# Block-sparse attention with a gated output: gathers moved behind both pairs' value products, query scaling moved behind the divisions

## The chip, the cores and the metric

One core of a Trainium2 chip. The metric is the device time of one execution in microseconds (us). The engines named below are TensorE (PE in the profile; PEld is its weight loads), VectorE (DVE), ScalarE (ACT), GpSimd (POOL) and SyncE (SP), which only issues transfers.

## The reference, cut to what matters

Batch 4, 8 heads, 768 positions, head size 64. Positions are in 24 blocks of 32. A block of queries sees the first and the last block, its own and both neighbours, and three blocks drawn at random; blocks 0 and 23 see everything.

```
scores = (q @ k^T) / 8, masked blockwise
attn   = softmax(scores)
x      = attn @ v                                  # heads side by side: 512 columns
gate   = sigmoid(causal convolution of x, 5 taps, one filter for each column)
out    = (gate * (x @ w_val)) @ w_out              # 512 x 512 weights
```

## The kernel before, in words

**Pairs and units.** The 22 inner query blocks of a batch are taken as 11 pairs of two neighbouring blocks. Blocks 0 and 23 form one more pair, the global one (`pr.glob`), which is worked in two halves. A unit is an inner pair or a half of a global one, 13 to a batch and 52 in all. `pr.seq` counts the inner pairs, 0 to 43.

**A unit's work.** `scores` multiplies the pair's queries (`qc`) by twelve blocks of keys (`kg`), takes the maxima on VectorE (`mx`) and the exponentials on ScalarE (`pe`). One step later `transposes` turns the exponentials on TensorE and ScalarE copies them out (`ptr`). `values` multiplies these by the values: `va` holds the first and last block and the pair's own two, which SyncE loads; `vb` holds, for each of the two query blocks, its other neighbour and its three drawn blocks, which POOL fetches by two indirect transfers of 128 rows (the gathers, `load_values`). The products go to `av`. VectorE then divides them by the row sums (`rs`, `x`). `finish` transposes the quotients (`xp`) into `xT`. A pair from batch 2 or 3 has 32 small products of values, each with 32 columns of weights and 65 columns of output; the profile shows each as two matmul records, 64 for a pair. In batches 0 and 1 (`wide`) pairs of products are joined where they can be, and there are 48 records.

**The gated output** runs in the gaps: `gates` (convolution on VectorE, tile `th`), `split` (`xh`, `xl`), and `project`, which issues on TensorE twelve products into `vp` for each quarter of the columns, evicts them by VectorE (`y`, `yl`) and ScalarE (`yh`), and then issues the output products `op`, in lots of six. The strings `FILLS` and `STEPS` say how many lots of TensorE work (`fill`) and of VectorE work (`prepare`) go in behind each transposed tile.

**Order.** Each engine is wrapped in `InOrder`, so its instructions run in the order in which the program issues them. Up to unit 21 a step takes one unit. From `DOUBLE_AT` = 22 on (the while loop at line 791) a step takes two inner units at once, or one unit around a global pair. Such a step is, in the program's order:

1. scale the queries of the next step's units (line 798, `SCALE_AHEAD` = 2), in place, on ScalarE for batches 0 and 1 and on VectorE for batches 2 and 3;
2. issue stores that are ready (SyncE);
3. scores of this step's units, with maxima and exponentials;
4. loads of later queries and keys (SyncE), and copies of keys into `kg` (POOL, and others) for the units of the next step;
5. values of the units of the step before (`to_value`), each with its division on VectorE;
6. value loads for the pairs three further on (`VRING` = 3): SyncE for `va`, POOL for the gathers;
7. further loads of queries and keys, transposes of this step's units with lots of projection and gate work between them, and the transposes of the quotients.

The buffers that set the waits: `vb` has three, so the gathers of pair s + 3 write the buffer that the products of pair s read. In a two-unit step, then, the two gathers of the first pair loaded wait for the first pair's products, and the two of the second for the second's. `va` and `kg` are rings of three and four, `qc` has five buffers.

Of the kernel before, what the change touches and what calls it, by code (L numbers as in the profile page):

```python
# [35 lines left out]
SCALE_AHEAD = 2  # L36
# [27 lines left out]
def attention_moe(ctx, tc, qb, kb, v, ve, sampled, w_val, conv_w, w_out, ident_in, slot_in, out):  # L64
# [29 lines left out]
    pe, dve, act, pool, sp = (InOrder(e) for e in (nc.tensor, nc.vector, nc.scalar, nc.gpsimd, nc.sync))  # L94
    matmul, transpose = pe.matmul, pe.transpose
# [55 lines left out]
    def indices(b):  # L151

        row = const.tile([128, NB], F32, tag=f"row{b % 2}", name="row")
        dve.tensor_scalar_add(row, base, float(b * S - B * S))
        dve.tensor_tensor(out=row, in0=row, in1=valid, op=ALU.mult)
        dve.tensor_scalar_add(idx[:, b, :], row, float(B * S))
# [18 lines left out]
    def run(calls):  # L175
        while calls:
            calls.pop(0)()
# [160 lines left out]
    def load_values(pr):  # L338
        b = pr.bt.b
        if pr.glob:  # L340
            return
        if pr.p == 0 and b:
            indices(b)
        vt = va[pr.seq % VRING]
        pr.va = vt
        if pr.p < VRING:
            sp.dma_start(vt[0 : 2 * BLK, :], ve[b])
        i0 = PAIRS[pr.p][0]
        sp.dma_start(vt[64:128, :], v[b * S + i0 * BLK : b * S + (i0 + 2) * BLK, :])
        pr.vb = three.tile([128, 2, H * DV], F32, tag="vb", name="vb")  # L350
        for j, i in enumerate(PAIRS[pr.p]):
            pool.indirect_dma_start(
                out=pr.vb[:, j, :], out_offset=None, in_=v,
                in_offset=bass.IndirectOffsetOnAxis(ap=idx[:, b, i : i + 1], axis=0),
            )


    class Unit:
# [65 lines left out]
    def transposes(un, places=((ps_pt, "pt"),) * 3):  # L424
        un.PT = []
        for p, (space, tag) in zip(un.P, places):
            pt = space.tile([128, 4, 128], F32, tag=tag, name="pt")
            for c in range(4):
                transpose(pt[:, c, :], p[:, 128 * c : 128 * c + 128], ident)
            t = five.tile([128, 4, 128], F32, tag="ptr", name="ptr")  # L430
            act.copy(t, pt)
            un.PT += [t[:, c, :] for c in range(4)]
            yield

    def values(un, second=False):
        pr = un.pr
        if un.e == 0 and second:
            pr.av = ps_pt.tile([128, 512], F32, tag="pt", name="av")[:, 0 : 4 * DV].rearrange(
                "p (a h d) -> p a h d", a=2, h=2
            )  # L440
        elif un.e == 0:
            pr.av = ps_av.tile([128, 2, 2, DV], F32, tag="av", name="av")
        if pr.glob:
            for h in range(2):
                for c in range(6):
                    pt = un.PT[4 * h + c if c < 4 else 4 + 2 * h + c]
                    for hp in range(HP):
                        cols = slice(BLK * hp, BLK * hp + BLK)
                        hd = 2 * hp + h
                        matmul(  # L450
                            pr.av[cols, un.e, h, :], pt[:, cols], pr.bt.vn[:, c, hd * DV : (hd + 1) * DV],
                            start=c == 0, stop=c == 5, tile_position=(0, BLK * hp),
                        )
        else:
            slots = [(a, h, b, (4 * a + 2 * b + h) * DV) for a in range(2) for h in range(2) for b in range(2)]
            wide = pr.bt.b < WIDE
            if wide:
                for a, h, b, hd in slots:
                    matmul(
                        pr.av[64 * b : 64 * b + 64, a, h, :], un.PT[4 * h + 2 * a][:, 64 * b : 64 * b + 64],  # L460
                        pr.va[:, hd : hd + DV], start=a + h == 0, stop=False, tile_position=(0, 64 * b),
                    )
            for a, h, b, hd in slots:
                for c in range(1 if wide else 0, 2):
                    for j in range(2):
                        rows = slice(64 * b + BLK * j, 64 * b + BLK * j + BLK)
                        vt = pr.vb[:, j, :] if c else pr.va
                        matmul(
                            pr.av[rows, a, h, :], un.PT[4 * h + 2 * a + c][:, rows], vt[:, hd : hd + DV],
                            start=c == 0, stop=a + h == 2 if wide else c == 1, tile_position=(0, rows.start),  # L470
                        )
        if un.last:
            rs = three.tile([128, 2, 2, 2], F32, tag="rs", name="rs")
            dve.tensor_scalar_add(rs[:, 0], pr.av[:, :, :, D], 1e-9)
            dve.reciprocal(rs[:, 1], rs[:, 0])
            pr.x = two.tile([128, 2, 2, D], F32, tag="x", name="x")
            dve.tensor_tensor(
                out=pr.x, in0=pr.av[:, :, :, 0:D], in1=rs[:, 1, :, :, None].to_broadcast([128, 2, 2, D]), op=ALU.mult
            )
# [163 lines left out]
    def store():  # L643
        while stores:
            sp.dma_start(*stores.pop(0))
# [30 lines left out]
    def fill(times=1):  # L676
        for _ in range(times):
            if may_project():
                run(late)
                advance(to_project)  # L680
# [21 lines left out]
    def freed(k):  # L702

        return units[min(k, N - 1)].pr.seq if k >= 0 else -1

    def more(which, upto, load):
        if at[which] < len(pairs) and pairs[at[which]].seq <= upto:
            load(pairs[at[which]])
            at[which] += 1
            return True  # L710

    def until(which, n, do):
        while at[which] < min(len(pairs), pairs.index(units[min(n, N - 1)].pr) + 1):
            do(pairs[at[which]])
            at[which] += 1
# [7 lines left out]
    for n in range(DOUBLE_AT):  # L723
# [5 lines left out]
        def more_values():  # L729
            return more("values", freed(n - LAG_V - 1) + VRING, load_values)  # L730
# [57 lines left out]
    to_value = units[DOUBLE_AT - LAG_V : DOUBLE_AT - LAG_T]  # L788
    to_finish = [un.pr for un in units[DOUBLE_AT - LAG_X : DOUBLE_AT - LAG_V] if un.last]
    n = DOUBLE_AT  # L790
    while n < N or to_turn or to_value or to_finish:
        step[0] = n
        now = units[n : n + 1]
        if n > DOUBLE_AT and len(units[n : n + 2]) == 2 and not any(un.pr.glob for un in units[n : n + 2]):
            now = units[n : n + 2]
        n += len(now)
        last = n - 1
        until("scaled", last + SCALE_AHEAD, scale)
        store()
        for i, un in enumerate(now):  # L800
            scores(un, i == 1)
        while now and more("keys", now[0].pr.seq + RING, load_keys):
            pass
        until("copied", last + COPY_AHEAD, copy_keys)
        for i, un in enumerate(to_value):
            values(un, i == 1)
            if un.last:
                to_finish.append(un.pr)
        if to_value:
            while more("values", to_value[-1].pr.seq + VRING, load_values):  # L810
                pass
        while more("keys", freed(last) + RING, load_keys):
            pass
        run(waiting)
        run(copies)

        def finish_pairs():
            if not to_finish:
                return
            xp = ps_pt.tile([128, 4, 128], F32, tag="pt", name="xp")  # L820
            ends = [finish(pr, xp[:, 2 * i : 2 * i + 2, :]) for i, pr in enumerate(to_finish)]
            for _ in range(2):
                for end in ends:
                    next(end, None)
            to_finish.clear()

        to_turn += now
        places = [(ps_sc, "sc")] * 3 + [(ps_pt, "pt")]
        count, done = sum(len(un.P) for un in to_turn), 0
        if len(to_turn) < 2:  # L830
            k = units.index(to_turn[0]) if to_turn else last + 1
            fill(int(FILLS[2 * k]))
            finish_pairs()
        for un in to_turn:
            k = units.index(un)
            step[0] = k
            for half, _ in enumerate(transposes(un, places[done : done + len(un.P)])):
                done += 1
                if done == count:
                    finish_pairs()  # L840
                at_half = 2 * k + min(half, 1)
                if len(to_turn) > 1 or half:
                    fill(int(FILLS[at_half]))
                prepare(int(STEPS[at_half]))
        to_value, to_turn = to_turn, []
# [54 lines left out]
```

## Time and profile before

| | |
|---|---|
| median of 3 runs | 402.89 us (402.58 to 407.91) |
| the profiled execution | 405.32 us, span 403.6 us |
| TensorE busy | 359.4 us (89%) |
| VectorE busy | 268.5 us (67%) |
| ScalarE busy | 255.5 us (63%) |
| POOL busy | 143.0 us (35%) |
| mean granted TensorE clock | 0.977 |
| chain of waits | TensorE 63%, VectorE 12%, issue 8%, ScalarE 7%, transfers 6% |
| gathers (vb) on POOL | 88, mean 983 ns |

Busy time is a share of the whole span. The chain of waits follows the work that ended last back to the start; "issue" in it is time in which an engine waited for nothing that the profile shows. A timeline row gives the start of its first instruction, the time from there to the end of its last, the engine, the line (of a helper, so always 82), the operation and its tiles, how many instructions the row holds, and in brackets the idle time of the engine ahead of them and what ended it. Matmuls are pipelined: a row of four can begin before the row ahead of it has ended. [...]

### The profile page before, as it was taken

Reading aid. Unit: us, or ns where it says so; the run is one execution under the profiler, and the core shown is the slowest. Engines: PE = TensorE matmul, PEld = TensorE weight load, DVE = VectorE, ACT = ScalarE, POOL = GpSimd, SP = SyncE. Lnnn points to the kernel's source line nnn. Section 1 sums busy time; section 2 is a strip of 40 time slices with the busy share of each in tenths; the row PEclk is TensorE's granted clock in tenths of the full one; section 3 lists DMA queues with packets and bytes.
Section 4 is the critical chain, followed back from the end, with each engine's and each line's share of the span. In section 5 each row is a group of like instructions: output and inputs, shape, how many; then the busy total and the mean of one; then the engine's idle time right before and its main releaser. Section 6 shows DMA issues by size and latency. Waiting matters only on the chain.

```text
span 403.6 us, 15476 instructions
## 1 busy us (share of the span) xinstructions
PE 359.4 (89%) x6274; PEld 286.4 (71%) x6274; DVE 268.5 (67%) x618; ACT 255.5 (63%) x619; POOL 143.0 (35%) x237
## 2 busy tenths in 40 slices
PE   8788889799789899697889988898999988999995
PEld 7356666566557788496668976696778867989794
DVE  4345798776978695375838856756755966779640
ACT  1958788788779567255648567755655866564521
POOL 1885656485733333503241051513351043000000
PEclk9989999999989999979989999999999999999999
DMA  7988966899944455968753676797660374101102
GB/s 229 302 287 262 325 224 169 229 297 320 306 141 103 123 153 114 298 207 236 218 148 104 175 185 165 210 310 218 188 185 18 89 203 137 53 28 54 52 26 81
DMA packets 52584, 72.37 MB, mean 179 GB/s; under 512 B 6944, under 2 KB 34720, under 8 KB 52512
## 3 DMA queue, kind: packets, MB, share of 16 engines
q1 hardware_dynamic: 44896, 47.69, 39.9%
q0 software_dynamic: 7040, 23.43, 20.1%
q8 instruction: 50, 0.82, 0.9%
q10 hardware_dynamic: 576, 0.24, 0.2%
q14 instruction: 22, 0.18, 0.2%
HBM read 65.05 MB, written 6.29 MB: 177 GB/s over the span
## 4 chain that ended last, share of the span: by engine, by line
PE 63%; DVE 12%; issue 8%; ACT 7%; DMA 6%; SPq 2%; POOL 1%; ACTq 0%; POOLq 0%; DVEq 0%
PE vp L82 14%; PE op L82 14%; PE av L82 14%; PE pt L82 10%; PE sc L82 7%; DVE mx L82 3%; DVE th L82 3%; PE s L82 3%; PE xp L82 2%; DMA qc<-in_q 2%; SPq L82 2%; ACT ptr L82 2%; DMA k<-in_k 2%; ACT pe L82 2%; DMA vb<-in_v,idx 2%
## 5 line engine op out<-in xcount | busy, mean ns | idle before, releaser
L82 POOL DMA_INDIRECT vb<-in_v,idx x88 | 86.5, 983 | 166.8 <-PE av L82 124.1
L82 DVE SCALAR_TENSOR_TENSOR th<-xT,cw,th 128x384 f32<-128x384 f32 x128 | 79.4, 629 | 24.5 <-ACT th L82 19.1
L82 ACT ACTIVATE pe<-sc,mx 128x256 f32<-128x256 f32 x176 | 67.9, 487 | 37.4 <-DVE mx L82 31.3
L82 ACT COPY ptr<-pt 128x512 f32<-128x512 f32 x112 | 64.2, 604 | 36.9 <-PE pt L82 28.4
L82 DVE TENSOR_REDUCE mx<-sc 128x2 f32<-128x512 f32 x88 | 55.5, 684 | 28.2 <-PE sc L82 16.9
L82 POOL COPY kg<-k 128x256 f32<-128x256 f32 (+1 forms) x143 | 55.9, 430 | 32.7 <-PE sc L82 24.0
L82 PE MATMUL av<-va,ptr 128*32 128x65 f32 (+1 forms) x1056 | 46.2, 226 | 11.7 <-issue 9.9
L82 PE MATMUL sc<-kg,qc 64*32 64x256 f32 x1408 | 52.5, 391 | 4.1 <-DVE rs L82 1.3
L82 PEld LDWEIGHTS av<-va,ptr 128*32 128x32 f32 (+1 forms) x1056 | 34.7, 118 | 29.5 <-issue 21.4
L82 PE MATMUL av<-vb,ptr 128*32 128x65 f32 x1408 | 44.0, 222 | 12.3 <-issue 11.0
L82 PE MATMUL op<-wo,yh 128*128 128x512 f32 x192 | 54.6, 407 | 0.1
L82 PE MATMUL pt<-ident,pe 128*128 128x128 f32 x352 | 51.5, 282 | 2.4 <-ACT pe L82 1.7
L82 PE MATMUL vp<-xh,wv 128*128 128x384 f32 x256 | 52.9, 349 | 0.0
L82 PEld LDWEIGHTS pt<-ident,pe 128*128 128x128 f32 x352 | 41.7, 144 | 8.1 <-ACT pe L82 2.5
L82 PEld LDWEIGHTS vp<-xh,wv 128*128 128x128 f32 x256 | 45.4, 193 | 0.3
L82 PEld LDWEIGHTS av<-vb,ptr 128*32 128x32 f32 x1408 | 32.8, 109 | 17.7 <-issue 14.5
L82 PEld LDWEIGHTS sc<-kg,qc 64*32 64x32 f32 x1408 | 27.1, 108 | 21.1 <-issue 9.6
L82 PEld LDWEIGHTS op<-wo,yh 128*128 128x128 f32 x192 | 35.4, 192 | 7.6 <-ACT yh L82 0.5
L82 ACT CAST yh<-y 128x384 fp32r<-128x384 f32 x32 | 16.5, 517 | 24.2 <-DVE y L82 23.0
L82 PE MATMUL op<-wo,yl 128*128 128x512 f32 x96 | 31.5, 409 | 0.0
L82 PE MATMUL vp<-xl,wv 128*128 128x384 f32 x128 | 28.0, 341 | 0.0
L82 DVE SCALAR_TENSOR_TENSOR y<-th,vp 128x384 f32<-128x384 f32 x32 | 17.6, 549 | 14.6 <-PE vp L82 14.6
(68 smaller groups left out, 433.2 us busy)
## 6 DMA issues: line engine op xcount, KB each, us to landing
kg<-in_k SPq DMA_DIRECT2D x165, 64.0 KB
vn<-in_v SPq DMA_DIRECT2D x12, 520.0 KB
qc<-in_q SPq DMA_DIRECT2D x48, 128.0 KB
k<-in_k SPq DMA_DIRECT2D x12, 512.0 KB
out<-ot SPq DMA_DIRECT2D x23, 256.0 KB
va<-in_v SPq DMA_DIRECT2D x44, 130.0 KB
wst<-in_w_val SPq DMA_DIRECT2D x4, 512.0 KB
wst<-in_w_out SPq DMA_DIRECT2D x4, 512.0 KB
```

Source lines behind the costliest of these rows:

```text
L82: made = getattr(self.eng, name)(*args, **kwargs)
```

## The change

In a two-unit step the first gather is made to wait for the last matmul of the step's value products, that is for the second pair's too; the other gathers of the step stand behind it on POOL. `product` keeps the last value matmul issued, and `valued` hands it to the first gather of the step and is then cleared. Where only one unit's values are computed in a step, and in the steps of one unit before unit 22, nothing changes for gathers. The scaling of the next step's queries moves from the head of the step to behind the value loads, so that on its engine it comes behind this step's maxima (or exponentials) and behind the divisions. No work is added or taken away.

```
--- before.py
+++ after.py
@@ load_values
         for j, i in enumerate(PAIRS[pr.p]):
-            pool.indirect_dma_start(
+            made = pool.indirect_dma_start(
                 out=pr.vb[:, j, :], out_offset=None, in_=v,
                 in_offset=bass.IndirectOffsetOnAxis(ap=idx[:, b, i : i + 1], axis=0),
             )
+            if valued[0] is not None:
+                tc.add_manual_dep(
+                    made.ins, valued[0].name,
+                    mybir.DependencyInfo(mybir.DependencyClass.Sync, mybir.DependencyReason.DATA),
+                    reason="behind the value products",
+                )
+                valued[0] = None
@@ values (in both branches)
+    valued, product = [None], [None]
...
-                        matmul(
+                        product[0] = matmul(
...
-                        )
+                        ).ins
@@ the loop of two-unit steps
         n += len(now)
         last = n - 1
-        until("scaled", last + SCALE_AHEAD, scale)
         store()
         for i, un in enumerate(now):
             scores(un, i == 1)
...
         if to_value:
+            valued[0] = product[0] if len(to_value) > 1 else None
             while more("values", to_value[-1].pr.seq + VRING, load_values):
                 pass
+            valued[0] = None
+        until("scaled", last + SCALE_AHEAD, scale)
         while more("keys", freed(last) + RING, load_keys):
             pass
```

## Rows read from the trace of the kernel before

**Rows 1.** Waits of TensorE, 130 to 360 us: total us, times, longest.

```profile
PE av L82 <- issue: 17.3, 35, 2.7
```

**Rows 2.** Timeline of TensorE in one two-unit step.

```profile
230.58 0.33 PE L82 MATMUL av<-va,ptr 128*32 128x65 f32 x8
...
232.62 0.22 PE L82 MATMUL av<-va,ptr 128*32 128x65 f32 x1 [0.16 <-issue]
...
234.09 0.33 PE L82 MATMUL av<-va,ptr 128*32 128x65 f32 x4 [0.43 <-issue]
...
234.82 0.33 PE L82 MATMUL av<-vb,ptr 128*32 128x65 f32 x4 [0.40 <-issue]
...
235.08 0.66 PE L82 MATMUL pt<-ident,pe 128*128 128x128 f32 x4
...
235.50 1.64 PE L82 MATMUL vp<-xh,wv 128*128 128x384 f32 x8
```

**Rows 3.** Timeline of POOL, 150 to 404 us: gathers.

```profile
157.23 0.97 POOL L82 DMA_INDIRECT vb<-in_v,idx  x1 [11.99 <-issue]
...
232.06 0.97 POOL L82 DMA_INDIRECT vb<-in_v,idx  x1 [12.23 <-PE av L82]
...
235.42 0.95 POOL L82 DMA_INDIRECT vb<-in_v,idx  x1 [1.15 <-PE av L82]
```

**Rows 4.** Timeline of TensorE, four other places.

```profile
152.55 0.69 PE L82 MATMUL av<-va,ptr 128*64 128x65 f32 x16
...
154.98 0.66 PE L82 MATMUL pt<-ident,pe 128*128 128x128 f32 x4
...
158.68 1.03 PE L82 MATMUL pt<-ident,pe 128*128 128x128 f32 x8
...
176.43 1.63 PE L82 MATMUL vp<-xh,wv 128*128 128x384 f32 x8
...
352.07 0.34 PE L82 MATMUL av<-va,ptr 128*32 128x65 f32 x8
...
354.04 1.66 PE L82 MATMUL op<-wo,yh 128*128 128x512 f32 x6
```

**Rows 5.** Timeline of TensorE: value products and next work, two steps.

```profile
183.99 0.33 PE L82 MATMUL av<-va,ptr 128*32 128x65 f32 x8
...
189.01 0.66 PE L82 MATMUL pt<-ident,pe 128*128 128x128 f32 x4
...
336.17 0.33 PE L82 MATMUL av<-va,ptr 128*32 128x65 f32 x8
...
340.41 0.60 PE L82 MATMUL pt<-ident,pe 128*128 128x128 f32 x4 [0.41 <-issue]
```

**Rows 6.** Timelines of VectorE and TensorE around 200 us.

```profile
199.92 0.15 DVE L82 TENSOR_SCALAR rs<-av 128x4 f32<-128x4 f32 x1
...
200.32 0.42 DVE L82 TENSOR_TENSOR x<-av,rs 128x256 f32<-128x256 f32 x1
...
203.79 1.82 PE L82 MATMUL pt<-ident,first 128*128 128x128 f32 x8
```

**Rows 7.** Timeline of TensorE, two steps around 135 and 165 us.

```profile
135.68 0.69 PE L82 MATMUL av<-va,ptr 128*64 128x65 f32 x16
...
140.35 1.64 PE L82 MATMUL vp<-xh,wv 128*128 128x384 f32 x8
...
164.56 0.69 PE L82 MATMUL av<-va,ptr 128*64 128x65 f32 x16
...
170.82 1.97 PE L82 MATMUL pt<-ident,pe 128*128 128x128 f32 x8 [1.70 <-ACT pe L82]
```

**Rows 8.** Timeline of VectorE, 120 to 172 us: one scaling.

```profile
169.00 0.29 DVE L82 TENSOR_SCALAR qc<-qc 128x256 f32<-128x256 f32 x1 [6.15 <-DMA qc<-in_q]
```

**Rows 9.** Busy us of PE, PEld, DVE, ACT, POOL; then clock, DMA share, GB/s.

```profile
163.00:182.10 19.10, 15.45 (x205) 14.15 (x205) 9.81 (x23) 8.12 (x19) 4.60 (x7) 0.82 0.86 247
182.10:195.30 13.20, 10.48 (x230) 8.89 (x230) 8.46 (x19) 8.25 (x20) 4.92 (x6) 1.00 0.82 238
```

More of the change, by code (lines that the diff above doesn't have):

```diff
@@ L467, in values @@
                         vt = pr.vb[:, j, :] if c else pr.va
-                        matmul(
+                        product[0] = matmul(
                             pr.av[rows, a, h, :], un.PT[4 * h + 2 * a + c][:, rows], vt[:, hd : hd + DV],
                             start=c == 0, stop=a + h == 2 if wide else c == 1, tile_position=(0, rows.start),
-                        )
+                        ).ins
         if un.last:
```

## The prediction

> **What bounds the kernel now.** I read the chain of waits first. Through the two-unit steps it is one run of TensorE work with short pieces called "issue" in it, so there whatever delays TensorE delays the end. The waits of TensorE alone, between 130 and 360 us, say what these pieces are: 17.3 us of idle time ahead of value products (av), with nothing named that it waited for; every other wait there is under 2 us in total, and none is for gathered rows [rows 1]. The timeline of TensorE then shows where in a step they lie. In the step whose value products begin at 230.58 the first pair and most of the second go through at full pace; a first gap ends at 232.62, and from there three or four products come at a time, 0.73 us apart (234.09 to 234.82), until the transposes begin at 235.08 [rows 2]. Beside it the reader should lay the timeline of POOL: the first gather of this step starts at 232.06, just ahead of that first gap [rows 2, 3].
>
> Two stretches decide whether the gather is the cause. In the step at 352.07 there is nothing left to gather: the products of two pairs (128 records) take 354.04 - 352.07 = **1.97 us**. In the step at 152.55 the gathers are late (they wait for new indices and start at 157.23): two pairs of the wide form take **2.43 us** [rows 3, 4]. Neither has a gap. In the other steps the same work takes 4.2 to 5 us. And what gathers do beside sparse work is there as well: gathers 3 and 4 of the 230.58 step run from 235.42 beside eight projections that take 1.64 us, against 1.63 us for eight at full clock with no gather [rows 2 to 4]; and under the four gathers from 157.23 eight transposes take 1.03 us [rows 3, 4]. So a gather costs TensorE only where TensorE issues very short products one upon the other.
>
> **The change part by part.**
>
> *Gathers behind the last value product.* It takes gathers 1 and 2 out of the second pair's products in eleven steps (the twelfth is the one at 152.55, already without them). Price of each: from the first value product to the next work, less the undisturbed time. Nine steps of 128 such records lie between 183.99 and 336.17: the first loses 189.01 - 183.99 - 1.97 = 3.05, the last 340.41 - 336.17 - 1.97 = 2.27, all nine 23.6 us [rows 5]. One of them can't give it all. At 197.69 TensorE goes straight to transposing the quotients, and those come from VectorE: it starts the first division at 199.92, each of two takes 0.82 us (to 200.74 for the first), so TensorE has them at 201.6 and its next transposes begin near 201.85 instead of 203.79, a gain of 1.9 and not 2.9 [rows 6]. That leaves 22.7. The step at 135.68 loses 140.35 - 135.68 - 2.43 - 0.42 (four transposes, as from 235.08 to 235.50) = 1.8 [rows 2, 4, 7]. Subtotal **24.5 us**.
>
> What the new wait holds up: behind the waiting gather stand, on POOL, the other three and then key copies. The first gather moves from 1.5 us after the first product (230.58 to 232.06) to about 2.3 us (1.97 and the 0.34 that gather 3 shows behind its product's end), so 0.8 us later against the step's start; the fourth ends about when it does today, since gathers 3 and 4 wait for the second pair already. Their rows are used one step on, a whole step later (the steps of rows 9 last 13 to 19 us), and by the program the copies behind them are for keys read at the scores of the step after the next. I cost this at nothing; the cover is that step of distance, and if it went, TensorE would wait for gathered rows, which it does nowhere after 130 us [rows 1, 3].
>
> *Queries scaled behind the maxima and divisions.* The scaling issues no DMA; SyncE's stores and key loads, POOL's copies and the value gathers, past which it moves in the program, run on other queues and keep their order. On VectorE 0.29 us for each query leaves the stretch ahead of the maxima and lands behind the divisions, ahead of the evictions of projections. In most steps both places are hidden under TensorE. In one, it decides: VectorE stood 6.15 us for a query load at 169.00 with the step's maxima behind it, so the exponentials came late and TensorE, done with its products, waited for them until 170.82 [rows 7, 8]. With the change those maxima run at once. The products begin at 164.56; one wide and one short pair take 2.2 us, so the transposes come near 166.8: **4.0 us** gained, gaps included. [...] Without the idle time I expect no fall, **2.6 us** more [rows 2, 4, 7, 9].
>
> *What is late next.* The ceiling is 24.5 + 4.0 + 2.6 = 31.1 us. Two things take from it. First, VectorE: the maxima and the first division now end while the products stand in their gaps; without them the second division (0.82) has to follow the first, and the scaling (0.29 to 0.6) comes behind it, so evictions start about 1 us later against the end of the products [rows 6, 8]. In two steps (183.99 and 230.58) output products follow one projection later and need its eviction: I take 0.5 each, **1.0** (bounds 0 and 2). Second, the transfers: from 163.00 to 195.30 the DMA engines are busy 0.86 x 19.1 + 0.82 x 13.2 = 27.2 us, and this stretch would shrink from 32.3 to 22.6 [rows 9]. Loads are issued a step ahead, so part of the missing 4.6 us can be carried into the emptier stretch behind; bounds 0 and 4.6, I take **3.0**, since both windows are near full.
>
> Sum: 31.1 - 1.0 - 3.0 = **27 us**. The profiled execution (405.32 us, span 403.6) would become 378; it lies 2.4 us above the median of 402.89, so the forecast is **376 us**.
>
> **The rivals.**
>
> *A. The gaps stay (0.10).* The slow stretch could belong to a long run of short products, which uses up what was issued ahead, and fall together with the gather by the fixed order of the step. For it: both begin at the same place of nearly every step. Against: the two undisturbed stretches, of which one has all 128 [rows 4]. It isn't excluded, because that one follows a single unit's scores instead of two. Then only the step at 164.56 gains: the 1.70 us that TensorE stood ahead of 170.82, with the clock 4.3; **399 us** [rows 7]. [...]
>
> *B. Half of it comes back as other waits (0.16).* The four gathers, now in one row, slow the first transposes: at the pace of [rows 2], four in 0.73 us, eight transposes take 1.45 instead of 0.84, 0.6 in each of twelve steps, 7 us; and the transfers take their full 4.6. With VectorE's 1.0 this leaves 31 - 13 = 18; **385 us**. For it: the full DMA windows [rows 9]; against it, transposes and projections at full pace beside gathers [rows 2, 4].
>
> *C. Slower (0.03).* In its new place the scaling waits for its query load with the evictions behind it; TensorE then waits for evicted projections in place of issue gaps. Price up to the 6.15 us of [rows 8] each. It decides once this wait exceeds about 2.9 us in all twelve steps (27 lost and 8 more); **411 us**. Against it: the new place is 4 us later, and one wait of that size is found.
>
> *D. No new wait arises (0.01).* If the first gather already stood behind both pairs nothing would move. But gathers 1 and 3 start 3.4 us apart, one behind each pair [rows 3].
>
> **How the numbers follow.** Forecast 0.70, from 368 (the ceiling of 31, and 3 more if the step at 197.69 also keeps its clock and its quotients are early) to 383. With B to 389 the range holds somewhat over 8 in 10; A, C and D and the worst of B lie outside. A measurement here can tell about 2%, 8 us, from no change: the limit is 395. Forecast and B are faster, 0.86; A and D within, 0.11; C slower, 0.03.
>
> **What would show it.** In the trace after, value products of two pairs should take about 2 us in every two-unit step, with the first gather starting 0.3 us behind them and TensorE's issue time at value products between 130 and 360 us below 5 us. The four gathers should stand back to back, with projections of 1.64 us beside them. [...] The forecast is wrong if the gaps stay with no gather beside them (A), if they reappear at transposes, or if TensorE now waits for vb, kg or evictions (B, C).

## The result and the profile after

The change takes the median from 405.94 us (402.58 to 409.13) to **394.11 us** (392.62 to 398.94), five executions each: a ratio of 0.972, 95% interval [0.967, 0.977]. It is faster, by 11.8 us where 27 were forecast, and outside the range of 368 to 389. The profiled execution of after took 398.94 us (span 397.1, granted clock 0.973) and is the longest of the five; its rows are read below for what happens, the medians for how much. Ratios, here and below, compare the executions of each kernel that lie within 1.5% of its fastest, so they can differ from the ratio of the medians.

The idle time that the change was to remove is nearly gone. TensorE's waits between 130 and 360 us in after (total us, times, longest), the first two rows:

```profile
PE av L82 <- DMA va<-in_v: 12.0, 4, 3.7
PE av L82 <- issue: 2.1, 2, 1.6
```

The issue time at value products fell from 17.3 us to 2.1 [rows 1], as forecast. But the row above it is new: 12.0 us, in four waits, for the values that SyncE loads.

A step in the middle, in TensorE's timeline of after (start, time to the last end, engine, line, operation, count, idle time ahead of it):

```profile
224.93 0.33 PE L82 MATMUL av<-va,ptr 128*32 128x65 f32 x8
...
226.91 0.66 PE L82 MATMUL pt<-ident,pe 128*128 128x128 f32 x4
227.32 1.63 PE L82 MATMUL vp<-xh,wv 128*128 128x384 f32 x8
```

and POOL's beside it:

```profile
227.31 0.97 POOL L82 DMA_INDIRECT vb<-in_v,idx  x1 [13.13 <-PE av L82]
228.58 1.32 POOL L82 DMA_INDIRECT vb<-in_v,idx  x1 [0.30 <-issue]
230.21 1.29 POOL L82 DMA_INDIRECT vb<-in_v,idx  x1 [0.30 <-issue]
231.81 0.95 POOL L82 DMA_INDIRECT vb<-in_v,idx  x1 [0.30 <-issue]
...
240.46 0.97 POOL L82 DMA_INDIRECT vb<-in_v,idx  x1 [5.66 <-PE av L82]
```

The products of both pairs take 226.91 - 224.93 = 1.98 us here. That is the only one of the nine steps of 128 records in the sum where they do: in the other eight they take 2.70 to 6.42 us, with other waits in place of the old gaps. The four gathers stand in one row behind both pairs, and the projections beside the first two take 1.63 us for eight, as without a gather [rows 2 to 4]. The step near 163 us also went as forecast; TensorE and, below, VectorE:

```profile
162.76 0.69 PE L82 MATMUL av<-va,ptr 128*64 128x65 f32 x16
164.96 1.09 PE L82 MATMUL pt<-ident,pe 128*128 128x128 f32 x8
165.81 1.64 PE L82 MATMUL vp<-xh,wv 128*128 128x384 f32 x8
...
167.97 1.56 PE L82 MATMUL vp<-xh,wv 128*128 128x384 f32 x8
```

```profile
161.94 2.48 DVE L82 TENSOR_REDUCE mx<-sc 128x2 f32<-128x512 f32 x4 [1.45 <-PE sc L82]
165.87 0.56 DVE L82 TENSOR_SCALAR qc<-qc 128x256 f32<-128x256 f32 x2
```

From the first value product to the transposes it is 164.96 - 162.76 = 2.20 us, against 170.82 - 164.56 = 6.26 [rows 7]: 4.06 gained, 4.0 forecast. The maxima wait for scores alone, and the scaling stands behind the divisions with no wait for its load (6.15 us in [rows 8]). The granted clock from 163 to 173 us is 1.00: eight transposes and twelve projections take 167.97 - 164.96 = 3.0 us. In before they took 176.43 - 170.82 = 5.6 [rows 4, 7], at a granted clock of 0.50.

**The new wait.** TensorE one step further on, at 252.94:

```profile
252.94 0.46 PE L82 MATMUL av<-va,ptr 128*32 128x65 f32 x8 [3.38 <-DMA va<-in_v]
254.84 1.66 PE L82 MATMUL pt<-ident,pe 128*128 128x128 f32 x8
```

and what SyncE (its DMA queue, SPq) issues ahead of it:

```profile
230.07 3.85 SPq L82 DMA_DIRECT2D kg<-in_k  x6
234.02 1.12 SPq L82 DMA_DIRECT2D va<-in_v  x2
235.23 0.54 SPq L82 DMA_DIRECT2D qc<-in_q  x1
237.28 3.94 SPq L82 DMA_DIRECT2D kg<-in_k  x6
241.32 0.38 SPq L82 DMA_DIRECT2D out<-ot  x1
241.79 0.38 SPq L82 DMA_DIRECT2D qc<-in_q  x1
244.75 4.17 SPq L82 DMA_DIRECT2D kg<-in_k  x6
249.02 0.49 SPq L82 DMA_DIRECT2D va<-in_v  x1
```

TensorE is ready for the second pair at 252.94 - 3.38 = 249.56, and only at 249.02 does SyncE come to issue that pair's `va`. It issues nearly without a rest: its own waits between 225 and 253 us come to 0.9 us. For one pair it is six loads of drawn key blocks (3.85 to 4.17 us), one of queries (0.4 to 0.5), `va` (half of 1.12), and ahead of the key loads 1.5 to 2.6 us that no row of this view names (the longest from 242.17 to 244.75). The operations on the tile of block numbers fill most of it; columns are count, then shortest, median and longest ns:

```profile
L290 SPq TENSOR_LOAD <-sm x33: 666/1272/2685, 53.5 to 318.0; - x33
```

For each pair SyncE reads six block numbers into registers, 1.27 us in the median, and then issues key loads with them: 6.5 to 7.5 us a pair, 13 to 15 for a step of two. The first gathers behind the products of two successive steps, at 227.31 and 240.46, are 13.2 us apart: in this stretch SyncE has no slack. Nor could it work ahead: stores stand in the same queue, and between 200 and 225 us SyncE waits 10.3 us for the outputs (`ot`) that it has to store. The chain of waits of after, around it (start, us, what):

```profile
249.02 3.78 DMA va<-in_v
252.80 0.14 issue
252.94 1.98 PE av L82 x64
```

Behind the idle time the clock falls: eight transposes take 1.66 us from 254.84 against 1.03 [rows 4]. The stretches of after around this wait (us, then busy time of PE, PEld, DVE, ACT, POOL; clock, DMA share, GB/s) show it:

```profile
252.00:255.00 3.00, 2.06 (x65) 1.92 (x66) 0.00 (x0) 0.06 (x1) 0.00 (x0) 0.61 0.37 101
255.00:258.00 3.00, 3.00 (x18) 3.00 (x19) 1.76 (x6) 1.56 (x3) 2.13 (x3) 0.82 0.59 158
```

### The profile page after: what moved, and what is told of

It reads as the page before. It is cut to its first block, busy times and chain, and to the rows that moved or that the text cites. A ratio compares the mean times of both kernels' runs of the same rounds, so it can differ in the third digit from the quotient of the medians.

```text
span 397.1 us, 15481 instructions
## 1 busy us (share of the span) xinstructions
PE 355.8 (90%) x6274; PEld 285.0 (72%) x6274; DVE 268.3 (68%) x618; ACT 255.1 (64%) x619; POOL 144.2 (36%) x237
## 4 chain that ended last, share of the span: by engine, by line
PE 66%; DVE 14%; ACT 8%; DMA 6%; issue 4%; SPq 1%; ACTq 0%; POOL 0%; POOLq 0%; DVEq 0%
PE op L82 16%; PE vp L82 14%; PE av L82 12%; PE pt L82 11%; PE sc L82 9%; DVE mx L82 4%; DMA va<-in_v 4%; DVE th L82 3%; PE s L82 3%; PE xp L82 2%; DMA k<-in_k 2%; ACT pe L82 2%; ACT ptr L82 2%; DVE wst L82 1%; DVE xl L82 1%
## 5 line engine op out<-in xcount | busy, mean ns | idle before, releaser
L82 POOL DMA_INDIRECT vb<-in_v,idx x88 | 89.2, 1014 | 165.8 <-PE av L82 132.6
L82 POOL COPY kg<-k 128x256 f32<-128x256 f32 (+1 forms) x143 | 54.3, 420 | 28.6 <-PE sc L82 19.7
L82 PE MATMUL av<-va,ptr 128*32 128x65 f32 (+1 forms) x1056 | 44.0, 233 | 19.2 <-DMA va<-in_v 12.0
L82 PE MATMUL op<-wo,yh 128*128 128x512 f32 x192 | 55.8, 414 | 0.1
L82 PE MATMUL av<-vb,ptr 128*32 128x65 f32 x1408 | 40.7, 227 | 4.6 <-issue 4.4
```

The lines of the kernel that those rows point to most:

```text
L82: made = getattr(self.eng, name)(*args, **kwargs)
```

## The experiments

In the seven comparisons of this study the kernel before falls into two kinds. In three (the first measurement and two of those below) it takes 403 to 406 us; in four, 388 to 390. I call them the 404 jobs and the 389 jobs; ratios are taken within a job only. One chip number occurs in both kinds, so the number of the chip doesn't decide it.

### Each part alone, and the order of SyncE (a 389 job; before 390.09 us)

The change again: no edit.

> The changed kernel once more, for a profile beside its rounds. All theories: 392 to 395 us. Queue theory (SyncE issues its loads back to back and the values of the second pair, va, come late): TensorE's waits for va at value products total about 12 us in the two-unit steps, and SyncE's issues stand with gaps under 0.5 us from 220 to 250 us. Gap theory (the old gaps stayed): issue time at value products stays above 15 us.

388.48 us, ratio 0.989 [0.983, 0.996]: on this job the change is worth about 1% (the medians are 0.4% apart), not 2.8. Its waits for `va` are 11.6 us in five pieces.

Gathers alone, the scaling put back in front:

```
         last = n - 1
+        until("scaled", last + SCALE_AHEAD, scale)
         store()
...
-        until("scaled", last + SCALE_AHEAD, scale)
```

> Only the gathers are moved; the scaling stays at the head of the step. Queue theory: the gaps go and waits for va take their place as in the full change, and VectorE's wait of 6 us for a query near 165 us stays: 396 to 401 us. If the two parts gain apart from each other and the scaling is worth its forecast 6.6 us: about 400. If the queue sets the end whatever VectorE does: 393 to 395, as with both parts.

392.41 us, 1.000 [0.993, 1.008]: nothing.

Scaling alone:

```
-            valued[0] = product[0] if len(to_value) > 1 else None
+            valued[0] = None
```

> Only the scaling is moved; the gathers wait as before the change. The gaps of about 2.5 us at value products stay in all steps. If the scaling alone removes the stop near 165 us (1.7 us and the clock behind it): 398 to 400 us. If it only works together with the gathers: 402 to 404.

389.34 us, 0.986 [0.977, 0.996], no less than the whole change gives here. But the medians, 389.34 and 390.09, are only 0.2% apart, so a gain of 1.4% isn't shown. Its gathers begin beside products as before, and none of the gaps expected comes (the step at 220.88 takes 2.09 us for its products); it waits 12.4 us for `va`.

The change with the first lot of key loads issued behind the value loads:

```
-        while now and more("keys", now[0].pr.seq + RING, load_keys):
-            pass
...
         until("scaled", last + SCALE_AHEAD, scale)
+        while now and more("keys", now[0].pr.seq + RING, load_keys):
+            pass
```

> Both parts, and the first lot of query and key loads of a two-unit step is issued behind the value loads instead of ahead of them, so that va leaves SyncE some 6 us earlier in the step; number and size of all transfers stay. Order theory (va is late only because it stands behind key loads): waits for va fall from 12 us to under 3 and nothing takes their place, 378 to 384 us. Pace theory (SyncE needs about as long for two pairs as the step lasts): waits of like size appear elsewhere, for keys or queries, 390 to 396 us. Transfer theory (the transfers themselves are too slow): va waits stay, 392 to 396.

383.53 us, 0.988 [0.981, 0.996], and 10.8 us of waiting for `va` still. The order within SyncE's queue is not the whole cause; if the queue is late as a whole, another order only makes something else late. The run alone doesn't settle it: in its chain of waits `va` lands 6.3 to 7.6 us after its issue, against 2.9 to 3.8 in after.

### Is it SyncE's pace or the bytes? (a 389 job; before 388.09 us)

Before again: no edit.

> The kernel before once more, for a profile beside these rounds, since it ran at 390 us beside the first four experiments and at 403 to 409 beside the change's first rounds. If the slow products beside the gathers belong to the kernel: eleven two-unit steps with 2.3 to 3 us of issue gaps at value products, 17 us in all. If they belong to single executions or to the chip: few such gaps, and in their place waits for va as in the changed kernel, 8 to 12 us in all.

387.87 us, 0.998 [0.993, 1.002]. Its profile shows a first gather beside products; POOL, then TensorE:

```profile
228.35 0.97 POOL L82 DMA_INDIRECT vb<-in_v,idx  x1 [12.22 <-PE av L82]
229.62 0.95 POOL L82 DMA_INDIRECT vb<-in_v,idx  x1 [0.30 <-issue]
```

```profile
226.87 0.34 PE L82 MATMUL av<-va,ptr 128*32 128x65 f32 x8
228.94 0.66 PE L82 MATMUL pt<-ident,pe 128*128 128x128 f32 x4
```

228.94 - 226.87 = 2.07 us: none of the gaps of [rows 2], although the gather starts 0.6 us ahead of the end.

Two of the six drawn key blocks of each pair in batches 2 and 3 copied by POOL from a batch's keys in SBUF, in place of being loaded by SyncE; the change otherwise:

```
-COPIED = [..., {}, {}]
+COPIED = [..., {0: POOL, 1: POOL}, {0: POOL, 1: POOL}]
```

> The change, and of the six drawn key blocks of a pair in batches 2 and 3 two are copied by POOL from the batch's keys in SBUF instead of loaded by SyncE: 88 loads fewer. Pace theory (SyncE's issues set the end): SyncE is relieved by about 1.1 us for a pair, 2.2 of some 14 us for a step, the waits for va at value products fall from 12 us to 3 or less, and the time falls by 6 to 14 us against the change alone, to 375 to 383. If the late values come from something else than SyncE's pace: within 3 us of the change alone, 385 to 390. If POOL becomes the bound: slower than the change alone, above 391.

379.08 us, 0.975 [0.968, 0.982]. No wait for `va` is left. The loads of key blocks fall from 165 to 121, by 44 and not by the 88 of the expectation. Over the whole run SyncE waits 93.1 us for outputs that it has to store, against 77.0 in after: it now has some time to spare.

The same with the value loads issued first, as in the run with the other order above:

> As the run with two blocks copied by POOL, and the value loads issued ahead of the step's first lot of key loads. Pace theory: about as the run without that, 373 to 383, no wait for va left. Order theory: clearly below it by 4 us or more.

379.23 us, 0.973 [0.965, 0.980]: the order adds nothing.

The change with as many loads, each of a quarter of the columns:

```
-            sp.dma_start(pr.kg[:, place, :], kb[:, b, bass.ds(reg, 1), :]...)
+            sp.dma_start(pr.kg[:, place, 0:32], kb[:, b, bass.ds(reg, 1), 0:32]...)
```

> The change, with each drawn key block that SyncE loads cut to its first 32 of 128 columns (the rest of the tile keeps older keys, so the scores are of other keys): as many issues, 48 KB less each. Pace theory: waits for va stay at 8 to 12 us and the time is within 3 us of the change alone. Transfer theory (the transfers are too slow, not their issue): waits for va fall below 4 us and the time falls by 6 us or more.

385.34 us, 0.996 [0.991, 1.001], and TensorE's first wait stands, here between 130 and 360 us:

```profile
PE av L82 <- DMA va<-in_v: 10.2, 4, 3.1
```

Six key loads still take 3.0 to 4.2 us of SyncE here (four rows from 215.98 to 240.58 us). A quarter of the bytes leaves the waits; a third fewer issues takes them away. **It is the time that SyncE needs to issue, not the transfers.** The block numbers in the run with two copies:

```profile
L290 SPq TENSOR_LOAD <-sm x33: 667/870/1252, 49.3 to 297.9; - x33
```

Four numbers cost 0.87 us where six cost 1.27, 0.20 for each.

### Is either part worth anything once SyncE is relieved? (a 389 job; before 389.39 us)

The two copies with the scaling alone, with neither part, and three copies with both:

> The kernel before with the scaling moved as in the change, the gathers left where they were, and two of the key blocks of each pair in batches 2 and 3 copied by POOL instead of loaded by SyncE. Pace theory (SyncE's issuing bounds the two-unit steps, and gathers beside products cost TensorE nothing): as the full change with the same two copies, a ratio of 0.975 (0.97 to 0.98), no waits for va, value products of two pairs in 2.0 us although a gather starts beside them. Gather theory (a gather beside short products slows them, hidden so far by the wait for va): once the va waits are gone the slow products appear, 1 to 3 us a step, and the ratio is 0.99 to 1.01.

> The kernel before, gathers and scaling as they were, with the two copies by POOL alone. Pace theory: its waits for va (3.3 us in the last profile of this kernel) and part of the wait for keys go, and its query loads are issued sooner, so that the scaling's stop of 4.7 us shrinks too: a ratio of 0.985 to 0.99, and the scaling's place is then worth no more than 1% beside the run with the scaling moved. If the scaling's place is worth its 1.3% for itself, this run stays at 0.99 to 1.0 and the stop of about 4.7 us on VectorE stays as well.

> The full change with three key blocks of each pair in batches 2 and 3 copied by POOL instead of two. Pace theory: SyncE was already faster than the step with two taken from it, so a third gives it nothing more, while POOL, which carries the four gathers of a step as well, gets longer: a ratio of 0.97 to 0.98, as with two. If SyncE is still the bound with two, another 0.5%: 0.968 or less. If POOL becomes the bound, TensorE waits for kg or vb and the ratio is above 0.985.

376.67 us, 0.968 [0.961, 0.975]; 377.75 us, 0.972 [0.964, 0.980]; 376.51 us, 0.971 [0.964, 0.978]. They can't be told apart. The copies alone give 2.8%, more than the 1.5% that I expected, and the two parts of the change add nothing to them that is clear of noise: the scaling's stop had been SyncE's late query load (VectorE stood 4.71 us for it near 165 us and 5.68 near 254 in the last profile of before; with the copies alone one such wait is left, 1.50 us near 238). A third copy gives nothing either, as the pace theory has it.

### Do gathers slow short products at all? (a 404 job; before 403.49 us)

The first gather made to start beside the first value product, with a fourth buffer for gathered rows, in the kernel before with the two copies:

```
+            valued[0] = product[0]          # here the first product of the step
             while more("values", ...
-        pr.vb = three.tile(...)
+        pr.vb = gath.tile(...)              # four buffers; pr and ptr have four, not five
```

> The kernel before with the two copies by POOL, one more buffer for gathered rows (room for it comes from one buffer less each of exponentials and of transposed exponentials), and the first gather of a two-unit step made to wait for the first value product of the step, so that two gathers of about 1 us each run wholly beside the 128 short products and not only beside their last 0.4 us. Gather theory (a gather slows short products wherever it runs, and showed little on this and the other chips because it began so late): products of two pairs take 3 to 5 us in place of 2.0 in the eleven steps, 12 us or more in all, a ratio of 1.0 or above. If a gather costs TensorE nothing: 2.0 us a step, and the ratio of the same kernel without this, 0.972 (0.965 to 0.98).

> Only the gathers moved, once more, on whatever chip it falls to. If the kernel before runs at 388 to 390 us here, as in the three jobs so far, the move is worth nothing again: 0.993 to 1.007. If it runs at 403 to 409 us, as in the first measurement, the slow products are there, and the gather theory gives 0.96 to 0.975 for this run; if the slow products had another cause than the gathers, 0.99 to 1.0.

> Only the scaling moved, once more, beside the run above. At 388 to 390 us for the kernel before: 0.985 to 0.99 again. At 403 to 409 us: with the gathers where they were the profile shows products in threes and fours, 0.73 us apart, behind the start of each first gather, 15 to 17 us in all, and a ratio of 0.985 to 0.99, if the gathers cause them; without such rows the slow products of the first profile belonged to that execution alone.

This job was of the other kind, and here the gathers matter: **437.39 us, 1.088 [1.081, 1.094]**, with the gathers under the products; 394.22 us, 0.980 [0.974, 0.986], with the gathers alone moved, somewhat less than the 0.96 to 0.975 expected; 402.22 us, 0.999 [0.995, 1.003], with the scaling alone, where 0.985 to 0.99 was expected. POOL and TensorE of the first of them:

```profile
243.96 0.97 POOL L84 DMA_INDIRECT vb<-in_v,idx  x1 [10.57 <-PE av L84]
245.23 0.94 POOL L84 DMA_INDIRECT vb<-in_v,idx  x1 [0.30 <-issue]
```

```profile
243.38 0.33 PE L84 MATMUL av<-va,ptr 128*32 128x65 f32 x8
...
244.54 0.22 PE L84 MATMUL av<-va,ptr 128*32 128x65 f32 x1 [0.17 <-issue]
244.57 0.23 PE L84 MATMUL av<-vb,ptr 128*32 128x65 f32 x1
245.27 0.27 PE L84 MATMUL av<-vb,ptr 128*32 128x65 f32 x2 [0.47 <-issue]
246.00 0.24 PE L84 MATMUL av<-vb,ptr 128*32 128x65 f32 x1 [0.46 <-issue]
...
250.40 0.66 PE L84 MATMUL pt<-ident,pe 128*128 128x128 f32 x4
```

The products go in eights until just behind the gather's start, then two to four at a time, 0.73 us apart; between the second gather (245.23 to 246.17) and the third (from 247.34) they run at full pace again, from 246.75 to 247.5. The step takes 250.40 - 243.38 = 7.0 us in place of 2.0. The rhythm is that of [rows 2]. With the scaling alone it is there too, in the same place as in before: 14.0 us of issue time at value products in 33 pieces; with the gathers alone 3.9, and in its place two others:

```profile
PE av L82 <- DMA va<-in_v: 4.9, 3, 3.1
PE pt L82 <- ACT pe L82: 4.2, 3, 1.8
PE av L82 <- issue: 3.9, 3, 1.8
```

### The same on another chip (a 389 job; before 388.82 us)

> The full change with two key blocks of each pair copied by POOL, once more. On a chip where the kernel before takes 403 us (slow products beside gathers): with SyncE relieved, nothing stands in the way of the gathers' gain, and the run reaches 377 to 381 us as on the other chips, a ratio of 0.935 to 0.945, 22 us or more, near the 27 that the sum forecast. Where before takes 388 to 390: 0.97 to 0.98 again. If the slow products came from something that the copies don't touch, 0.955 or more on the 403-us chip.

> The kernel before with the two copies alone, once more. On a 403-us chip the slow products stay, since the gathers still begin beside them: 0.975 to 0.99, and 12 us or more behind the run above. On the others 0.968 to 0.975 and no distance to the run above.

> Gathers wholly beside the products, once more. On a 403-us chip 1.08 to 1.095 again, products trickling from the first gather on. On the other kind of chip: if a gather slows short products there as well, and the kernel before only got away with it because its first gather begins when 0.45 us of products are left, 1.06 to 1.12 and the same trickle; if those chips do not know the effect, 0.965 to 0.985 and products of two pairs in 2.0 us.

379.56 us, 0.986 [0.979, 0.993]; 375.00 us, 0.972 [0.963, 0.982]; 377.86 us, 0.980 [0.972, 0.989]. The kernel that took 437 us takes 378 here; POOL and TensorE:

```profile
219.73 0.97 POOL L84 DMA_INDIRECT vb<-in_v,idx  x1 [10.56 <-PE av L84]
```

```profile
219.16 0.33 PE L84 MATMUL av<-va,ptr 128*32 128x65 f32 x8
221.54 0.66 PE L84 MATMUL pt<-ident,pe 128*128 128x128 f32 x4
```

2.38 us with one gather wholly beside the products and the next, from 221.00, for its first half: 0.4 more than without, where the other job lost 5. The effect isn't missed by tenths of a microsecond in the 389 jobs; it is not there in that size.

### The change with the copies, in a 404 job (before 406.12 us)

> The full change with the two copies by POOL, a third time. On a 403-us chip: if only SyncE kept the gathers' gain back there, 377 to 381 us, a ratio of 0.935 to 0.945; if something else than SyncE keeps it back, 0.955 or more. On the other kind of chip 0.97 to 0.99, and this stays open.

387.14 us, **0.954 [0.949, 0.959]**: 19 us, between what I had written for the two theories. TensorE's waits before 130 us, and then between 130 and 360:

```profile
PE av L82 <- issue: 6.1, 15, 1.2
```

```profile
PE av L82 <- issue: 7.5, 5, 3.6
PE xp L82 <- DVE x L82: 1.8, 2, 1.6
```

and a step of two units in its timeline of TensorE:

```profile
223.07 0.33 PE L82 MATMUL av<-va,ptr 128*32 128x65 f32 x8
225.05 0.66 PE L82 MATMUL pt<-ident,pe 128*128 128x128 f32 x4
```

Products of two pairs take 1.98 us, and nothing waits for `va`. The fifteen short waits before 130 us stand in steps of one unit, whose gathers the change leaves where they are. They come to about what this run lacks by then against the same kernel in a 389 job: the transposes that in [rows 4] begin at 154.98 begin at 154.22 here and at 148.04 there, 6.2 us apart, and the spans are 385.7 and 377.0, 8.7 apart; only 2.5 us of it arise in the steps behind.

## Why the prediction was wrong

**Gathers behind the last product, 24.5 us: the cause was right, where it occurs, and the price too high.** That a gather slows short products, and only those, was inferred from two undisturbed stretches. In a 404 job it is shown by moving the gathers either way: away from the products 0.980, under them 1.088 (a kernel that has the two copies and other buffers as well, but in a 389 job it is at 0.980). Each of the four 389 jobs has a profile with gathers beside products and without that slow pace, and in the one where the gathers alone were moved the term is zero (1.000 [0.993, 1.008]). From one profile I couldn't know that this is a property of the occasion, and the 24.5 us were booked as the kernel's own.

Not all of them were the gathers' in that profile either. The 3.05 us of the step at 183.99 are one single gap, and not the row of short ones, 0.73 us apart, that the gathers leave. TensorE has it again in the change with the copies in a 404 job, where the first gather of the step comes behind the products, at 183.35. First before, then that run:

```profile
188.42 0.25 PE L82 MATMUL av<-vb,ptr 128*32 128x65 f32 x2 [2.72 <-issue]
```

```profile
181.97 0.32 PE L82 MATMUL av<-vb,ptr 128*32 128x65 f32 x2 [3.64 <-issue]
```

A part of the loss at 323.16 is of this kind too (1.19 us of idle time ahead of 326.06; 1.02 at the same place in that run). The nine steps of 128 records, priced at 23.6 us over nine times the undisturbed 1.97 us, take 41.3 us for their products in the profile of before, 37.3 in that of after, and 29.1 in the change with the copies, in another 404 job: 4.0 us gained in after, 12.2 where nothing waits for `va`. Of the 19.6 us that after still loses there, 12.0 are waits for `va`, 2.1 issue and 1.5 waits for ScalarE; the rest is slower products behind them, such as the second pair from 252.94 to 254.84.

**The scaling, 4.0 + 2.6 us: right in the step, and given back.** The step gained 4.06 us and kept its clock: the 2.6 us in the sum are the fallen clock of before, 5.6 us for the transposes and projections at 0.50 against 3.0 in after at 1.00. Yet the scaling alone is worth 0.001 [-0.003, 0.005] of the time in the 404 job, and the 1.4% of a 389 job isn't shown by its medians. In after the very next step waits 3.69 us for `va`, the first of the four waits: what the step at 163 us gains SyncE doesn't.

**What is late next: this step failed.** I looked for the next limit among the transfers, by the busy share of the DMA engines (0.82 to 0.86 [rows 9]), and took 3.0 us of 4.6. The limit was SyncE, which issues them. I named its queue only to say that its order stays; I never added up what it has to do in a step: 13 to 15 us for two pairs, against steps that before lasted about as long with their gaps (products begin at 230.58, 245.55 and 258.53), and that should have shrunk by 2 to 3 us. The term measures 12.0 us of waits for `va` in after, and the clock behind them; quartering the bytes left 10.2 of it, a third fewer issues nothing. The sum with 12 in place of 3 gives 18 us; 11.8 were measured. The clock behind the four waits and the gaps that were never the gathers' take more; their shares were not told apart. With the copies, which take away this limit, the same change comes to 19 us in a 404 job. Not all of that is the change: what the copies alone give there wasn't run. In the first profile of before the wait for `va` doesn't show [rows 1]; that its gaps gave SyncE the time is argued, not shown.

**VectorE, 1.0 us:** no wait for an eviction is in after's list, so it is not refuted; it is too small to be shown.

**The rivals.** B had the right shape (half comes back as other waits) and the wrong place: the transposes behind the gathers and the projections beside them run at full pace (0.66 us for four and 1.63 for eight in the step at 224.93). Its other half, the transfers at their full 4.6 us, was the nearest to the truth, but it priced bytes. A was right for the single gaps above, which stay with no gather beside them. That gathers cost the products nothing is nearly what the 389 jobs look like (0.4 us with gathers under the products); the 404 job, with 5.0 us in one step, goes against it. C and D didn't occur.

**Open.** What makes a job of the one kind or the other; by which way a gather holds up the products in a 404 job; what the copies alone give there; and how much of SyncE's lateness comes from the stores in its queue, for whose outputs it waits 48.1 us between 130 and 360 us in after and 47.5 in before (no run moved them). What beats both kernels is the two copies: in the kernel before they take 0.972 of its time in two 389 jobs; with the change, 0.954 in a 404 job and 0.975 and 0.986 in 389 jobs. Where a kernel has to run on both kinds, the copies with the gathers moved look like the safer choice, since the gathers alone give 0.980 in a 404 job; the two weren't compared there, and in one 389 job they stood 4.6 us behind the copies alone.

## What to carry to other kernels

When a change is to shorten steps, add up for every queue, the issuing ones too, what it has to do in a step, and compare that with the step's new length: a queue that is just in time today can be without a row among the waits (TensorE has none for `va` between 130 and 360 us in the first profile of before, and 12.0 us of them in after). The busy share of the DMA engines said nothing here about the engine that issues. Price only losses that have the pattern of their cause: one gap of 2.72 us is not a row of gaps 0.73 us apart. And look whether a stall that is read from one execution is there in another before it is priced.

## What was not expected of the hardware

- One kernel took 437 us in one job and 378 in another. Of the 56 us between the spans of the two profiles (433.7 and 378.0) 39 stand at the products of ten two-unit steps, with gathers beside products of 65 columns.
- A load at a drawn address costs SyncE about 0.33 us (median of 165) and, for the address, 0.20 us in a register load. Six key loads with what goes between them take 3.85 to 4.17 us and the register load 1.27: together most of a pair's 6.5 to 7.5 us.
- TensorE's long issue waits at products (0.4 to 4.7 us each) come back in most of these kernels at the same places of its instruction stream: ahead of about the 5826th, 6338th, 11202nd and 11714th of all its records in the trace, weight loads and matmuls counted alike. These places are 512, 4864 and 512 records apart, all multiples of 256. The single gaps of before at 168.01, 188.42 and 326.06 are the first three. What causes them was not tested.
